# Row length of five zero fills on the software DMA queue: fills 25, 26, 27, 29 and 30 written in 56 KB rows

## The chip, the cores and the metric

One core of one Trainium2 chip. The metric is the device time of one execution in microseconds (us), less is better. Six runs of the kernel before lie between 766.58 and 799.4 us, with a median of 774.3 us.

## What is computed

The program is the forward and backward pass of one decode step: a layer norm, an attention block A over a sliding window of a key/value cache, a gate from a small dense block B with a squared ReLU, and `x + s * g`; the outputs are the result and the gradients of all inputs.

```python
W = min(4096, max(256, Sk // 4))           # Sk = 32768, so W = 4096
k = jnp.repeat(k_cache[:, :, Sk - W:, :], rep, axis=1)
v = jnp.repeat(v_cache[:, :, Sk - W:, :], rep, axis=1)
p = _softmax(scores, axis=-1)
...
s = _A_ref(xn, A_k_cache, A_v_cache, A_wq, A_wo)
g = _silu(_B_ref(xn, B_w1, B_b1, B_w2, B_b2))
return x + s * g
```

Only the last 4,096 of 32,768 cache rows are used. The gradients of both caches (`out_2`, `out_3`; 2 batches x 8 heads x 32,768 rows x 128 bf16 each) are therefore zero in the first 28,672 rows of each head. These zeros are 32 pieces of 7.34 MB, 234.9 MB in all, out of 280.50 MB that the program writes.

## The kernel before

**Zero fills.** `zt` (line 80) is a tile of 128 x 14,336 bytes of zeros. The helper `zf` (line 90) writes one piece, or a part of it, from that tile by a DMA on POOL's software queue (line 101), and lets the DMA convert the bytes on the way: the destination is read as bf16, so that one tile row becomes 28,672 bytes of output, or, where a row would be longer than the tile's, as fp32, so that one tile row becomes 57,344 bytes. The loop at line 115 issues pieces ("fills") 0 to 30 in order of number. A fill whose number is in `zlong` (line 107) is written in 128 rows of 57,344 bytes ("long"); one that is not is written in 256 rows of 28,672 bytes ("short"); fills 2, 4, 6, 8 and 10 are cut into parts of several sizes by `zshort` (line 108). In the order of the queue, the last ones are: 16 to 19 long, 20 and 21 short, 22 to 24 long, 25 to 27 short, 28 long, 29 and 30 short. They make 47 DMAs. The queue has eight semaphores, so POOL issues a DMA when the one eight places before it has landed; the last one is issued at 553.65 us of the profile, and the queue is never empty before that. Fill 31 is written at the very end, by SP (line 623): it is issued after SP's last other store and waits for the landing of fill 29 (line 624).

**Attention.** After the weights, four rounds (the loop over `rounds`, two groups of four heads x two batches) each hold a V tile and a K tile of 4 MB, in one buffer each. A round computes scores with V and K (`scores`, lines 377 and 383), the softmax, the contractions (`contract`, line 399), then the gradients tile by tile *into the same buffer* (`outer_store`, line 410), and stores that buffer on ACT's queue (line 414): first V's, then K's. SP loads the next round's V (line 213) once V's store has landed, and K likewise. K and V rows go in 32,768-byte pieces, 128 of them to a tile. In the second and fourth rounds the gradient of `wq` is also formed, in place (line 495).

**Epilogue.** Line 498 gives the K/V buffers back, and the tiles of the epilogue (`epi`, line 499) are placed there: so `o_rows`, the first of them, is written only after the last K store has landed. The epilogue is one chain of small steps: `o_rows` (line 506), the output projection (line 515), the gate, the gradients of B (lines 555 to 590), then `dw2` (line 608) and its store on SP (610), `dw1` (616) and its store (618), fill 31 (623), and the gradient of `wo` (628) and its store on ACT's queue (630). The gradient of `wq` is stored by ACT at line 500.

Of the kernel before, what the change touches and what calls it, by code (L numbers as in the profile page):

```python
# [16 lines left out]
def kernel(  # L17
# [86 lines left out]
    ZQ = 2 * B * HKV  # L104
    zparts = [(out_2, q) for q in range(B * HKV)] + [(out_3, q) for q in range(B * HKV)]

    zlong = (3, 5, 7, 11, 12, 16, 17, 18, 19, 22, 23, 24, 28)
    zshort = {
        2: ((5, 8, 2), (120, 68, 3), (128, 32, 1), (16, 1, 1)),
        4: ((3, 1, 2), (2, 99, 6), (128, 112, 1), (128, 102, 1), (86, 1, 1)),  # L110
# [547 lines left out]
```

## Time and profile before

| what | value |
|---|---|
| six runs: times | 766.58, 766.74, 766.74, 781.86, 784.45, 799.4 us |
| six runs: median | 774.3 us |
| the profiled execution: its own time | 800.91 us |
| the profiled execution: span, first to last instruction | 799.1 us |
| PE, DVE, ACT, POOL busy | 415.2 (52%), 277.2 (35%), 214.9 (27%), 30.2 us (4%) |
| bytes moved by DMA | 326.73 MB, mean 409 GB/s |
| of these by the software queue | 227.55 MB in 8000 packets |
| last V store: issued, landed | 648.61, 684.57 us |
| last K store: issued, landed | 677.56, 702.66 us |
| store of `dw2` issued | 758.53 us |
| fill 31 issued, landed | 765.90, 796.94 us |

The profile is one execution, the longest of those listed. Times in it are counted from its first instruction. A "packet" is one piece that a DMA engine moves in one go; in this trace a packet of the fills is one row (28,672 or 57,344 bytes), and one of the K and V transfers is 32,768 bytes. Sixteen DMA engines serve all queues: q0 is POOL's software queue, q1 is SP's, q10 is ACT's. The page cuts the span in 40 slices of 20 us; the digits are tenths of busy time, and the row GB/s is what the DMA engines moved in each slice.

### The profile page before, as it was taken

The page shows a single profiled execution, that of the slowest core. Times are in us where ns is not written, and L with a number is a line of the kernel's source. Part 1 is how long each engine was busy: PE and PEld are TensorE (multiplying, and loading weights), DVE is VectorE, ACT ScalarE, POOL GpSimd, SP SyncE. Part 2 cuts the span into 40 slices and gives each one's busy share as a digit, 9 for nine tenths or more (in the row PEclk, how much of TensorE's full clock was granted, in tenths as well). Part 3 has the DMA queues.
Part 4 walks back from the last instruction along what each step waited for, and adds up shares of the span by engine and source line. Part 5 has one row for each costly group of instructions (what it writes and reads, how often), then busy time and mean ns, then how long its engine had stood idle before and what let it go on. Part 6 is the DMA issues. An engine that isn't in the chain of part 4 may idle for free.

```text
span 799.1 us, 9402 instructions
## 1 busy us (share of the span) xinstructions
PE 415.2 (52%) x4118; PEld 269.3 (34%) x4118; DVE 277.2 (35%) x484; ACT 214.9 (27%) x313; POOL 30.2 (4%) x56
## 2 busy tenths in 40 slices
PE   0275873747503757750583578102517587275690
PEld 0253462634102645420362443002516443134230
DVE  3034241355401437440141375201204554113770
ACT  0024431145500235450120256100102465120260
POOL 3000000010000100000000000000000000000000
PEclk9997897868755996675576968655959587556555
DMA  9999999999999999999999999999999999993089
GB/s 358 433 432 418 444 422 434 423 450 412 429 431 435 428 437 424 427 433 434 436 435 437 428 419 433 432 438 429 442 418 431 429 443 420 434 432 150 1 367 394
DMA packets 12473, 326.73 MB, mean 409 GB/s; under 512 B 2276, under 2 KB 2284, under 8 KB 2294
## 3 DMA queue, kind: packets, MB, share of 16 engines
q0 software_dynamic: 8000, 227.55, 67.3%
q1 hardware_dynamic: 2696, 56.63, 19.9%
q10 hardware_dynamic: 1736, 41.95, 12.4%
q8 instruction: 32, 0.52, 0.2%
q14 instruction: 9, 0.07, 0.0%
HBM read 45.62 MB, written 280.50 MB: 408 GB/s over the span
## 4 chain that ended last, share of the span: by engine, by line
DMA 37%; PE 32%; DVE 13%; ACT 7%; issue 4%; another core or an unknown queue 3%; ACTq 0%; DVEq 0%; SPq 0%
DMA out_dram<-nat 14%; DMA nat<-in_A_k_cache_dram 10%; DMA nat<-in_A_v_cache_dram 9%; PE ov L410 6%; PE s_ps L383 4%; PE tp L377 4%; DMA b_bf<-in_B_b_dram 4%; DVE tT L156 3%; PE dp_ps L383 2%; ACT p_bf L444 2%; DVE nat L156 2%; PE wps L628 2%; DVE ds_bf L457 2%; ACT tT L154 2%
## 5 line engine op out<-in xcount | busy, mean ns | idle before, releaser
L377 PE MATMUL tp<-pperm,nat 128*128 128x128 bf16 x1024 | 85.0, 234 | 175.7 <-DMA nat<-in_A_v_cache_dram 122.5
L156 DVE COPY tT<-tp 128x1024 bf16<-128x1024 bf16 x96 | 64.1, 689 | 242.1 <-PE tp L377 241.5
L377 PEld LDWEIGHTS <-nat 128*128 128x128 bf16 x1024 | 74.1, 106 | 182.2 <-DMA nat<-in_A_v_cache_dram 124.2
L154 ACT COPY tT<-tp 128x1024 bf16<-128x1024 bf16 x32 | 32.4, 1012 | 305.7 <-PE tp L377 305.7
L154 ACT CAST nat<-ov 128x512 bf16<-128x512 f32 x160 | 87.9, 589 | 60.9 <-PE ov L410 59.6
L156 DVE CAST nat<-ov 128x512 bf16<-128x512 f32 x96 | 65.4, 690 | 57.7 <-PE ov L410 56.9
L410 PE MATMUL ov<-bd,ds_bf 128*128 128x512 bf16 x128 | 52.2, 486 | 5.8 <-DVE nat L156 3.9
L410 PE MATMUL ov<-bd,p_bf 128*128 128x512 bf16 x128 | 47.4, 438 | 4.7 <-DVE nat L156 1.8
L383 PE MATMUL dp_ps<-tT,zdo 128*128 128x256 bf16 x256 | 42.2, 298 | 14.5 <-DVE tT L156 8.6
L101 POOL DMA_DIRECT2D out_dram<-zt x47 | 28.6, 613 | 524.1 <-DMA out_dram<-zt 520.8
L383 PE MATMUL s_ps<-tT,zq 128*128 128x256 bf16 x256 | 39.4, 280 | 13.9 <-DVE tT L156 9.2
L383 PEld LDWEIGHTS <-zdo 128*128 128x128 bf16 x256 | 25.8, 105 | 23.4 <-issue 19.8
L399 PE MATMUL ps<-t,nat 128*128 128x16 bf16 x1024 | 28.5, 173 | 9.4 <-DVE bd L367 7.8
L399 PEld LDWEIGHTS <-nat 128*128 128x128 bf16 x1024 | 28.4, 101 | 12.7 <-issue 7.6
L383 PEld LDWEIGHTS <-zq 128*128 128x128 bf16 x256 | 24.7, 100 | 20.9 <-issue 18.2
L495 PE MATMUL wps<-dq_rows,xn_bf 2*128 2x512 bf16 x32 | 14.9, 536 | 23.2 <-ACT wq L154 18.0
L391 PE MATMUL tp<-ident_bf,p_bf 128*128 128x128 bf16 x64 | 7.6, 313 | 34.9 <-ACT p_bf L444 34.9
L444 ACT ACTIVATE p_bf<-e_sb,rl 32x512 bf16<-32x512 f32 x16 | 22.8, 1423 | 3.4 <-DVE rl L441 3.3
L156 DVE CAST wq<-wps 128x512 bf16<-128x512 f32 x16 | 11.0, 690 | 31.6 <-PE wps L495 31.2
L457 DVE SCALAR_TENSOR_TENSOR ds_bf<-dp_ps,delta,p_bf 32x512 bf16<-32x512 f32 x16 | 21.7, 1358 | 0.2
L410 PEld LDWEIGHTS <-ds_bf 128*128 128x128 bf16 x128 | 13.6, 113 | 23.0 <-issue 20.7
L154 ACT CAST dw_st<-wps 128x512 bf16<-128x512 f32 x15 | 8.8, 585 | 46.4 <-PE wps L608 43.7
(197 smaller groups left out, 454.7 us busy)
## 6 DMA issues: line engine op xcount, KB each, us to landing
out_dram<-zt POOLq DMA_DIRECT2D x26, 7168.0 KB, 162.4
out_dram<-nat ACTq DMA_DIRECT2D x8, 4096.0 KB, 32.9
nat<-in_A_v_cache_dram SPq DMA_DIRECT2D x4, 4096.0 KB, 34.1
nat<-in_A_k_cache_dram SPq DMA_DIRECT2D x4, 4096.0 KB, 38.2
out_dram<-zt POOLq DMA_DIRECT2D x4, 3584.0 KB, 56.6
out_dram<-zt SPq DMA_DIRECT2D x1, 7168.0 KB, 31.0
out_dram<-zt POOLq DMA_DIRECT2D x1, 6120.0 KB, 85.9
wo<-in_A_wo_dram SPq DMA_DIRECT2D x1, 4096.0 KB, 38.3
```

The lines of the kernel that those rows point to most:

```text
L101: sw_fill.append(nc.gpsimd.dma_start(out=v, in_=zs))
L154: nc.scalar.copy(out=out_ap, in_=in_ap)
L156: nc.vector.tensor_copy(out=out_ap, in_=in_ap)
L377: nc.tensor.transpose(tp[:, j, :], nat[:, g * CC + half * CH + j, :], pperm[:].rearrange("p b k -> p (b k)"))
L383: nc.tensor.matmul(out_ps[:, half * CH * PB:(half + 1) * CH * PB], lhsT=zbuf[:, pr, o:o + R], rhs=tT[:, :, pr, :], start=(g == 0 and pr == ...
L391: nc.tensor.transpose(tp[:, cc, :], src[:, half * CH + cc].rearrange("r k b -> r (k b)"), ident_bf[:, :])
L399: nc.tensor.matmul(ps[:], lhsT=nat[:, g * CC + half * CH + cc, :], rhs=cols[half][:, cc, :, g, :], start=(half == 0 and g == 0 and cc == 0 ...
L410: nc.tensor.matmul(ov[:], lhsT=src[:, cc].rearrange("r k b -> r (k b)"), rhs=bd[:, gh * 4:(gh + 1) * 4, :], start=True, stop=True)
L444: nc.scalar.activation(out=p_bf[rb, :, :, pr], in_=e_sb[rb], func=ACT.Copy, scale=rl[rb, 0:1])
L457: nc.vector.scalar_tensor_tensor(out=ds_bf[rb, :, :, pr], in0=dp_c[rb], scalar=delta[rb, 0:1], in1=p_bf[rb, :, :, pr], op0=ALU.subtract, o ...
L495: nc.tensor.matmul(wps[:], lhsT=xn_bf[:, k:D:DK], rhs=dq_rows[:, :], start=True, stop=True)
L628: nc.tensor.matmul(wps[:], lhsT=o_rows[:, j:N:NJ], rhs=ds_rows[:, :], start=True, stop=True)
```

## The change

Five numbers are added to the tuple of long fills; nothing else is touched.

```diff
-    zlong = (3, 5, 7, 11, 12, 16, 17, 18, 19, 22, 23, 24, 28)
+    zlong = (3, 5, 7, 11, 12, 16, 17, 18, 19, 22, 23, 24, 25, 26, 27, 28, 29, 30)
```

For these five, `whole` at line 117 is `(128, 224, 1)` in place of `(128, 112, 2)`: one DMA each as before, of 128 rows of 57,344 bytes in place of 256 rows of 28,672. All fills from 22 to 30 are then long. The number of DMAs, their order, their semaphores, and the instructions of all other engines stay as they are; fill 31 still waits for fill 29.

## The prediction

> **What bounds the kernel now.** I read the page's 40 slices first, then busy times by stage, the DMA queues in short windows, the chain of work that ended last, and the waits. The slices:
>
> ```profile
> DMA  9999999999999999999999999999999999993089
> GB/s 358 433 432 418 444 422 434 423 450 412 429 431 435 428 437 424 427 433 434 436 435 437 428 419 433 432 438 429 442 418 431 429 443 420 434 432 150 1 367 394
> ```
>
> The DMA engines are full from 20 us to about 727 us at some 430 GB/s; then comes one hole, which the stages show (columns: busy us and count for PE, PEld, DVE, ACT, POOL, then PE clock, DMA share, GB/s):
>
> ```profile
> 597.00:648.00 51.00, 36.84 (x417) 26.83 (x416) 27.00 (x44) 22.20 (x31) 0.00 (x0) 0.80 1.03 435
> ...
> 728.00:758.00 30.00, 18.94 (x178) 11.32 (x176) 17.77 (x27) 4.10 (x7) 0.52 (x1) 0.50 0.01 2
> 758.00:800.00 42.00, 20.94 (x48) 6.55 (x47) 15.78 (x25) 14.04 (x24) 0.00 (x0) 0.50 0.85 362
> ```
>
> The hole is 30 us with 2 GB/s: the fills are used up, and the epilogue has not yet made what is left to store. The execution took 800.9 us; without the hole it would be about 771. That lies near the lowest three of the six runs (766.6 to 766.7, within 0.2 us of each other), so I read those as runs without a hole: DMA engines full to the end, and nothing to gain but bytes. The other three (781.9, 784.5, 799.4) have holes of 15 to 33 us. The time is the later of two ends: that of the bytes, 766.7, and that of the chain.
>
> Where the chain comes from, before the hole:
>
> ```profile
> 677.56 25.10 DMA out_dram<-nat
> 702.76 1.00 ACT o_rows L154
> ```
>
> ```profile
> ACT o_rows L154 <- DMA out_dram<-nat: 19.4, 1, 19.4
> ```
>
> The first epilogue step stands 19.4 us, until the last K store (issued 677.56) has landed at 702.66. From there, small steps follow without another DMA wait to the `dw2` store at 758.53 (55.9 us) and on to the end. So each us that this store lands later makes the hole, where there is one, a us longer.
>
> [...] Beside short fills, the last V store, and the last K store:
>
> ```profile
> q10 hardware_dynamic: 111, 3.54, 55.9%
> q0 software_dynamic: 109, 2.84, 44.4%
> ```
>
> ```profile
> q10 hardware_dynamic: 112, 3.67, 57.4%
> q0 software_dynamic: 112, 2.87, 44.8%
> ```
>
> (windows 664 to 679 and 685 to 700 us; packets, MB, share). 111 packets against 109, 112 against 112: one for one. Beside long fills, the last K load, 556 to 576 us:
>
> ```profile
> q0 software_dynamic: 96, 5.33, 62.1%
> q1 hardware_dynamic: 98, 3.21, 38.4%
> ```
>
> Again one for one, but now the fill takes 62% of the bytes. [...] the one issued at 544.09 landed at 596.77, 52.7 us later. [...]
>
> **The change, part by part.**
>
> *Fewer rows (removed).* 5 x 128 = 640 packets fewer. Fills that run alone show what a row length is worth: POOL's issues at 422.93, 439.68, 456.56, 473.48 and 490.42 mark the landings of fills 16 to 20. The long ones 17, 18, 19 took 16.75, 16.88 and 16.92 us, the short fill 20 took 16.94. At best 5 x 0.19 = 1 us, at worst nothing; I take 0. POOL's issue is 0.54 us for a long fill against about 0.71 for a short one, 0.9 us less over five, hidden: POOL stands 520.8 us waiting for landings.
>
> *Fills 25, 26, 27.* In this execution they run from 597 to 648 us, where the window shows 435 GB/s and the queue listing q0 alone. No other transfer competes: cost 0. Their cover is that the last round's loads have landed (596.77). If the chain runs some 25 us earlier, as it must where there is no hole, the last V store would start beside fill 26 or 27 instead of 28, and meet long rows there; the next two steps then apply a little earlier, at the same price.
>
> *Fill 29, beside the last V store.* The store moved nothing from 649 to 660 us, behind rows of fill 28, which is long already. From 664 it had 3.54 MB left, taking 15 us at 0.236 MB/us. Beside long rows the measured pace is 3.21/20 = 0.160 MB/us: 22.1 us, so 7 us later; last bytes at about 687 in place of 679.7.
>
> *Fills 29 and 30, beside the last K store.* It sits behind the V store on ACT's queue. Before, its first packet moved at 683.4; now it waits until 687: 3.7 us later. Its 4.19 MB took 4.19/0.245 = 17.1 us at 3.67/15; at 0.160 they take 26.2: 9.1 more. Fills 29 and 30 together, 14.7 MB at 5.33/20 = 0.267 MB/us from 664, last until 719, so they accompany the store to its end. Sum: 3.7 + 9.1 = 12.8 us. The late semaphore, which stores have shown as up to 4.9 us after the last packet, may add 0 to 5; a queue delay that is lighter than the pace of a load suggests may take off 4. I take 12, with bounds 8 and 18; a gain is excluded here, since no packet of a store moves sooner when those between are longer.
>
> *After that.* The landing goes to about 715, and all of the epilogue moves with it: `dw2` at 770, the end at 813 for the execution profiled. The `wq` store (issued 711.13) moves too, but finds no fill beside it, so it ends before `dw2`; 0. Fill 31 waits for fill 29, which lands earlier than before; SP reaches it only after the `dw1` store, so this frees nothing. No wait or instruction is added on PE, DVE, ACT or SP.
>
> **From the profiled execution to the median.** Runs with a hole pay all 12 us: 781.9 becomes 793.9, 784.5 becomes 796.5, 799.4 becomes 811.4. Runs at the floor pay what exceeds their slack, the time by which their chain ends early. No profile of such a run is here; slack is between 0 and, from the spread of the six, some 25 us. If it is 8 us, they go to 770.7. The median of six is then the middle of 770.7 and 793.9: 782 us.
>
> **Rivals.**
>
> *A, slack covers it (not slower).* In runs at the floor the chain may end over 12 us early; then the stores give up bytes to the fills and get them back at the end, the total being fixed, and the time stays 766.7. It decides from a slack of 12 us. For it: three runs within 0.2 us, which a chain close to the floor would have scattered. Against it: the other three are 15 to 33 us above, so the chain's own scatter is wider than the slack can be sure of. Time where most runs are at the floor: 767.
>
> *B, longer rows move more bytes (faster).* The 1 us above, or a hole that the fills' earlier end makes no longer. Faster by over 0.2% needs 1.5 us, more than the five fills can give by the rows measured. Only a floor that sinks, or a sample with fewer holes, would show it: 765.5.
>
> *C, late landing decides (much slower).* The load that landed 52.7 us after its issue was beside long rows. If the last stores, or in a late run the last K load beside fill 25, land some 10 us later yet, the median is 782 + 10 = 792, and single runs pass 815.
>
> That the change does nothing is no rival: the 13 long fills are in the trace with 57,344-byte packets by the same code.
>
> **Chances.** 0.2% (1.5 us) is about what a measurement can tell here. My forecast (some us up to 12) 0.52; C 0.12; A 0.28; B 0.08. So slower 0.64, same 0.28, faster 0.08. The range goes from A's floor, 766, to 798, which takes in most of C; about 1 in 10 is left out above and 1 in 10 below. The slower cases alone would give 770 to 798.
>
> **What would show it.** Right: beside fills 29 and 30 the q0 share near 62% and q10 at 0.16 MB/us; last K store 33 to 38 us from issue to landing in place of 25.10; ACT's wait at `o_rows` longer by that; a longer DMA hole, or a new one. Wrong: `o_rows` not waiting for the store, or a full DMA row up to the last slice with the stores late (A).

## The result and the profile after

The changed kernel takes 816.67 us in the median of 10 runs (799.12 to 818.3); the kernel before takes 774.34 us in the median of 20 (766.58 to 801.34). Over the runs of each kernel that lie within 1.5% of its fastest, the ratio is 1.0433, 95% interval [1.0418, 1.0448]: 33 us slower. The runs of both kernels fall in groups some 17 us apart (766.7, 783 and 800 before; 799 to 801 and 814 to 818 after). The execution profiled after belongs to the lower group (798.84 us, span 797.1), and the fourth round's K load lands at 562.8 us in it. So its fair partner is not the profile of 800.91 us that the prediction read, where that load lands at 596.77, but one of the kernel before at 766.96 us (`b_look1`), where it lands at 563.2.

The slices of the changed kernel's page:

```profile
DMA  9999999999999999999999999999999999994089
GB/s 357 434 429 425 434 434 433 420 443 417 436 430 429 437 437 415 438 426 429 436 439 435 430 423 426 430 435 436 440 432 433 423 434 421 446 424 189 1 368 395
```

and those of the kernel before in the run of 766.96 us:

```profile
DMA  9999999999999999999999999999999999999998
GB/s 356 429 429 427 443 416 429 444 424 425 427 435 430 430 445 435 418 425 432 432 433 441 427 430 428 430 432 433 437 435 431 419 432 432 435 428 425 427 429 367
```

The prediction read the lowest runs as runs without a hole, and so it is. The change puts a hole of some 30 us in. Two stretches of the changed kernel, the second being the hole (columns as before):

```profile
649.00:701.00 52.00, 5.69 (x39) 2.54 (x39) 4.70 (x9) 2.98 (x5) 0.00 (x0) 0.53 1.29 431
728.00:755.00 27.00, 17.56 (x164) 10.64 (x161) 15.95 (x25) 3.51 (x6) 0.00 (x0) 0.50 0.01 1
```

In the first of these 52 us every compute engine is nearly idle while the DMA engines are full: the epilogue waits for the last K store. The waits of the changed kernel, and of the kernel before at 766.96 us:

```profile
ACT o_rows L154 <- DMA out_dram<-nat: 47.2, 1, 47.2
```

```profile
ACT o_rows L154 <- DMA out_dram<-nat: 20.4, 1, 20.4
```

The chain that ended last, of the changed kernel from 590 us on:

```profile
600.92 6.00 issue
...
633.63 5.33 issue
...
654.11 47.08 another core or an unknown queue
701.29 1.00 ACT o_rows L154
```

and of the kernel before at 766.96 us:

```profile
638.62 25.47 DMA out_dram<-nat
664.19 1.00 ACT o_rows L154
```

Two things are new: two stretches in which PE waits for nothing that the profile shows ("issue", 11.3 us; the kernel before at 766.96 us has none of over 2.0 us), and the 47.08 us before `o_rows`, for which the chain names no cause. The last K store was issued at 648.94 and landed at 701.19. Its packets say where the time went. The table gives, from the trace's records, the time from issue to first packet, from there to the last packet (of the 128 of 32,768 bytes), and from that to landing, with the V store ahead of it on the same queue:

| store | issued | to first packet | packets move | last packet to landing | in all |
|---|---|---|---|---|---|
| last V, before, 800.91 us | 648.6 | 12.1 | 19.0 | 4.9 | 36.0 |
| last V, before, 766.96 us | 617.2 | 6.5 | 18.4 | 2.7 | 27.7 |
| last V, changed, 798.84 us | 621.0 | 12.0 | 25.0 | 4.8 | 41.8 |
| last K, before, 800.91 us | 677.6 | 5.9 | 18.1 | 1.2 | 25.1 |
| last K, before, 766.96 us | 638.6 | 5.6 | 18.5 | 1.4 | 25.5 |
| last K, changed, 798.84 us | 648.9 | 11.0 | 24.7 | 16.5 | 52.2 |

The V store is the clean measure of the start: nothing stands ahead of it on ACT's queue. When the K store was issued, the V store still moved, for another 2.1, 3.5 and 9.1 us in the three executions.

So the account of the lower groups, both counted from the landing of the fourth round's K load (563.2 and 562.8 us): V store issued 54.0 and 58.2 us later (+4.2), K store 21.5 and 28.0 after that (+6.5), landed 25.5 and 52.2 after that (+26.7), `dw2` 56.7 and 55.3 after that (-1.4). Sum +36.0; the times differ by 31.9, so some 4 us were slack. The +26.7 are 5.4 of start, 6.2 of moving packets and 15.1 of wait after the last packet.

The shares beside long rows, in windows 636 to 656 and 664 to 684 us of the changed kernel (V store, K store):

```profile
q0 software_dynamic: 98, 4.87, 56.7%
q10 hardware_dynamic: 108, 3.54, 42.5%
```

```profile
q0 software_dynamic: 109, 5.45, 63.2%
q10 hardware_dynamic: 107, 3.51, 41.8%
```

Still about one packet each (98 against 108, 109 against 107), and 3.51/20 = 0.176 MB/us for the store, near the 0.160 of the forecast.

### The profile page after: what moved, and what is told of

Same layout as the page of the kernel before. It is cut to its first block, busy times and chain, and to the rows that moved or that the text cites. A ratio compares the mean times of both kernels' runs of the same rounds, so it can differ in the third digit from the quotient of the medians.

```text
span 797.1 us, 9402 instructions
## 1 busy us (share of the span) xinstructions
PE 413.9 (52%) x4118; PEld 269.2 (34%) x4118; DVE 277.1 (35%) x484; ACT 214.7 (27%) x313; POOL 29.3 (4%) x56
## 4 chain that ended last, share of the span: by engine, by line
PE 32%; DMA 32%; DVE 15%; ACT 8%; another core or an unknown queue 6%; issue 5%; ACTq 0%; DVEq 0%; SPq 0%
DMA out_dram<-nat 11%; DMA nat<-in_A_k_cache_dram 9%; DMA nat<-in_A_v_cache_dram 8%; PE ov L410 5%; PE s_ps L383 4%; PE tp L377 4%; DMA b_bf<-in_B_b_dram 4%; DVE tT L156 3%; PE dp_ps L383 3%; DVE ds_bf L457 2%; ACT p_bf L444 2%; DVE nat L156 2%; PE wps L628 2%; PE dops L308 2%
## 5 line engine op out<-in xcount | busy, mean ns | idle before, releaser
L410 PE MATMUL ov<-bd,ds_bf 128*128 128x512 bf16 x128 | 49.8, 468 | 5.7 <-DVE nat L156 4.1
L410 PE MATMUL ov<-bd,p_bf 128*128 128x512 bf16 x128 | 49.7, 457 | 4.1 <-DVE nat L156 1.8
L383 PE MATMUL dp_ps<-tT,zdo 128*128 128x256 bf16 x256 | 41.3, 294 | 15.2 <-DVE tT L156 8.4
L101 POOL DMA_DIRECT2D out_dram<-zt x47 | 27.7, 594 | 534.4 <-DMA out_dram<-zt 531.2
L383 PEld LDWEIGHTS <-zdo 128*128 128x128 bf16 x256 | 25.5, 104 | 23.9 <-issue 20.6
L156 DVE CAST wq<-wps 128x512 bf16<-128x512 f32 x16 | 11.0, 690 | 58.6 <-PE wps L495 58.2
L483 PEld LDWEIGHTS <-wqT 128*128 128x128 bf16 x128 | 4.4, 101 | 52.1 <-issue 50.7
```

What stands on the lines that cost most here:

```text
L101: sw_fill.append(nc.gpsimd.dma_start(out=v, in_=zs))
L156: nc.vector.tensor_copy(out=out_ap, in_=in_ap)
L383: nc.tensor.matmul(out_ps[:, half * CH * PB:(half + 1) * CH * PB], lhsT=zbuf[:, pr, o:o + R], rhs=tT[:, :, pr, :], start=(g == 0 and pr == ...
L410: nc.tensor.matmul(ov[:], lhsT=src[:, cc].rearrange("r k b -> r (k b)"), rhs=bd[:, gh * 4:(gh + 1) * 4, :], start=True, stop=True)
```

## Experiments

In the traces of both kernels the records of a K or V store end with 16 packets of 4 bytes, called its completion writes here; the last K store of the changed kernel has 14 that took 12.7 to 14.8 us, the last of them ended at 700.85 us, the store landed at 701.19, and fill 29, in flight beside it, at 701.90. "Held" is said below of a completion write that lasts so long. Three theories, for the runs to test: **S** (the forecast's): only the shares of bytes count. **H1**: a completion write beside a long fill is held until that fill's DMA has ended. **H2**: it is held only as long as nothing else follows on its own queue. What the long fills have that the others lack is also split: the length of the row, or the conversion of the zeros to fp32 (each byte of the tile becomes four of output, called widening by 4; by 2 in a short row).

**e0_before_again**: the kernel before, no edit.

> The kernel before, unchanged, to see a run at the floor (766.7 us). Theory H (a load's or store's completion write is held until the long fill in flight has ended, up to 7 packets of 2.11 us): in such a run the last round runs some 25 us earlier than in the profile of before, the last K store starts near 645 to 650 us beside fill 27 or 28, and its landing comes at 670 to 680; the dw2 store is issued within some 5 us of the end of the fills and of the wq store (about 728), so there is little slack. Theory S (only the shares of bytes count, and the slack is used up by more than the forecast 12 us): the chain in a run at the floor ends close to the floor, slack 0, and the last K store takes 25 to 30 us.

Measured: 766.69 to 801.29 us in five runs; the profile is of the run of 801.29 and shows what the first profile showed, so it leaves the slack open. It shows where the group at 800 comes from, though: the fourth round's K load has its last packet at 581.6 us and lands at 596.8, with fill 24 (597.0).

**e1_long_25_27 and e2_long_29_30**: one part of the change each.

```diff
-    zlong = (3, 5, 7, 11, 12, 16, 17, 18, 19, 22, 23, 24, 28)
+    zlong = (3, 5, 7, 11, 12, 16, 17, 18, 19, 22, 23, 24, 25, 26, 27, 28)
```
```diff
+    zlong = (3, 5, 7, 11, 12, 16, 17, 18, 19, 22, 23, 24, 28, 29, 30)
```

> Fills 25, 26 and 27 long, 29 and 30 short. Theory H: the last K store lands while a short fill runs, or at the end of fill 28, so the wait after its last packet falls from 16.5 us to under 2 where fill 29 runs then; runs at about 780 to 788 us, 12 to 19 less than the changed kernel's lower runs (799). Theory S: the last V and K stores move beside fills 25 to 28 for most of their bytes, so most of the loss stays: 790 to 799 us.

> Fills 29 and 30 long, 25 to 27 short. Theory H: if the last K store's last packet moves during fill 28 or 29, its completion is held until that fill ends: landing near 700 us and runs near 795 to 800 us, though most of its bytes moved beside fills of before. Theory S: the V store is as quick as before, the K store only little slower: 770 to 778 us.

Measured: e1 784.57, 792.62, 801.39, 801.6 us; e2 782.86, 799.24, 816.14, 816.93. Against the lowest run of before, both parts cost about 17 us in theirs, and the whole about 32; but four runs can miss a group. In e1's profile (801.6) the last K store moves beside the short fill 29 and lands 23.9 us after its issue, as quickly as before, and PE stands 5.64 us in "issue" beside fill 27: the V store, issued 51.8 us after the K load's landing in the profile of before, is issued after 57.9. In e2's (816.14) that store takes 42.3: 12.3 to the first packet, 27.9 moving, 2.0 to land, at the very end of the fills (718.2, fill 30 at 718.4). S has e2 at 770 to 778 and fails for every run; H1's 795 to 800 holds for one of four. The parts do not act on the same thing: with 25 to 27 long, PE stops and the V store is issued later (57.9 us against 51.8), with 29 and 30 long the K store takes longer (42.3 us against 25.1).

In both profiles the fourth round's K load lands at 596.8 us, as in the profile of 800.91 us, so that is their partner. Beside it e1 costs 0.7 us: its V store starts sooner after its issue (10.1 us in place of 12.1), and the K store is issued 2.0 us later only. e2 costs 15.2, and nearly all of that is what the forecast counted: the V store moves 8.9 us longer, the K store starts 6.5 and moves 9.9 longer. In e2's profile the loss lies in when the packets start and how long they move, not in the 2.0 us after them.

**e3_f32_short**: the five fills in rows of 28,672 bytes, as before the change, but converted to fp32.

```diff
-    def zf(o, q, r0, nent, rows, rep=1):
+    def zf(o, q, r0, nent, rows, rep=1, as_f32=False):
...
-        if w > ZG * DH:
+        if as_f32 or w > ZG * DH:
...
-            r = zf(*zparts[qi], r, n, rows, rep)
+            r = zf(*zparts[qi], r, n, rows, rep, as_f32=qi in (25, 26, 27, 29, 30))
```

> The five fills in rows of 28,672 bytes as before, but converted to fp32 as the long ones are (7,168 bytes of the tile a row). If row length decides (H and S as stated): as the kernel before, 766.7 us in its lower runs. If the conversion to fp32 is what holds completions: the last K store lands up to 7 packets of 1.06 us late, so 774 to 780 us, with completion writes of several us in the trace.

Measured: 799.09, 799.14, 801.32, 818.33 us: the changed kernel's times, with the rows of the kernel before, and far from both expectations. So most of the loss comes with the conversion, not with the length. The equal times are in part chance: in e3's profile the K load lands at 574.5 us, 11.7 later than in the changed kernel's, and both K stores land with the end of fill 29, at 701.8 and 701.2. The V store beside these rows starts 11.9 us after its issue (12.0 in the changed kernel, 6.5 in the kernel before at 766.96 us), a time in which each engine moved some 11 packets of the fill instead of 5 or 6 (estimates: 167 packets on 16 engines in the 11 us from 632 in e3, 2.16 us for a long packet in the changed kernel, 1.08 for a short one); the K store's completion comes 13.3 us after its last packet (1.4 in the kernel before at 766.96 us); PE stands 5.34 and 4.04 us in "issue". Only the share is another matter; windows 672 to 687 us of e3, K store beside fp32 rows of 28,672 bytes:

```profile
q10 hardware_dynamic: 100, 3.28, 52.0%
q0 software_dynamic: 104, 3.01, 46.9%
```

3.28/15 = 0.219 MB/us, with about one packet each: the store's share goes with the row's length, as the forecast had it (52.0% here, 55.9 and 57.4% beside rows of this length in the kernel before, 41.8% beside 57,344 bytes in the changed kernel); the waits at both ends go with the conversion (11.9 and 13.3 us).

**e4_push and e4_look**: the changed kernel, with a small load right behind the last K store on ACT's queue.

```diff
+    push = const.tile([P, FK], BF16, name="push")
...
+        if r == NR - 1:
+            with tc.issue_after(st.ins):
+                dma_store.dma_start(out=push[:], in_=B_b1.rearrange("(p j) -> p j", j=FK))
```

> The changed kernel, with one small load (128 pieces of 28 bytes of B_b1, into a tile that nothing reads) issued on ACT's queue right after the last K store. Theory H2 (a completion write beside fp32 fills is held while nothing else follows on its queue, and passes after one or two fill packets if something does, as the last V store's did with the K store behind it): the K store's wait after its last packet falls from 16.5 us to 3 to 6, so 784 to 789 us in the lower runs (799 for the changed kernel). Theory H1 (it is held until the fp32 fill in flight has ended, whatever follows): no change, 799 and 817 us.

> The changed kernel with the small load behind the last K store, one look. Theory H2 (traffic behind a completion lets it pass): in a run at 789 to 792 us the wait after the last K store's last packet is under 7 us, where the changed kernel has 16.5. Theory H1 alone: a run at 799 us with 13 to 17 us of wait.

Measured: e4_push 789.51, 791.88, 817.23, 817.28 us; its profile (817.23) tells nothing of the hold, since there the K store lands at the end of all fills (719.1). e4_look's profile is of a run of 785.75 us: the wait after the last packet is 3.3 us where the changed kernel has 16.5, with fill 29 in flight until 702.3 and the landing at 688.3. So here, with something behind it on its queue, the store landed 14.0 us ahead of the fill. The last V store shows the same without any edit: in the changed kernel, with the K store's packets starting behind it, 14 of its 16 completion writes took 2.16 us, as long as one long packet (2.16); 14 of the 16 of the K store, with nothing behind it, took 12.7 to 14.8, as long as six or seven.

H2 as worded is wrong at two points, though. To stand in the queue was not enough in b_look2: the fourth round's K load was issued behind the V load at 542.7 us, its first packet moved at 551.0, and the V load's completion writes took up to 12.7 us and ended between 549.1 and 553.1, with fill 22. And the other transfer was not on the same queue in another case: in six profiles the third round's K store ended beside a long fill with nothing behind it, while a load moved on SP's queue (at 540.3 us in the profile of 800.91 us), and its completion writes took 0.01 us.

The profile of 817.23 us tells something else: its K load lands at 596.8 us, as in the profile of 800.91. So with the fills long a run of the group at 800 comes out at 817, 16 us later and not 33.

**e5_two_halves**: the changed kernel, each of the five fills as two DMAs of 64 long rows.

```diff
+        if qi in (25, 26, 27, 29, 30):
+            whole = (P // 2, ZR // P, 1)
...
-    tc.add_manual_dep(fin.ins, sw_fill[-2].ins.name,
+    tc.add_manual_dep(fin.ins, sw_fill[-3].ins.name,
```

Fill 31 waits for the second half of fill 29.

> The changed kernel, with each of the five fills as two DMAs of 64 long fp32 rows, so that a DMA has 4 packets on an engine instead of 8. Theory H1 (held until the end of the fill DMA in flight): at most 3 to 4 packets of 2.11 us are held, 6 to 8 us instead of 14.8, so about 791 us in the lower runs. [...]

Measured: 789.66, 799.7, 800.14, 817.59 us. In the profile (789.66) the K store's last packet ends at 684.6 and the store lands at 692.1, with the first half of fill 29 (692.8): 7.5 us instead of 16.5, and the completion writes took at most 6.4 us, three packets (14.8 in the changed kernel). This is H1's number, with 4 packets a DMA and engine in place of 8.

**e6_short_from_20**: all fills from 20 on short.

```diff
+    zlong = (3, 5, 7, 11, 12, 16, 17, 18, 19)
```

> All fills from 20 on in short bf16 rows, 22, 23, 24 and 28 too. If the fp32 fills 22 to 24 hold the fourth round's K load until a fill's end, and so set by how much each run exceeds 766.7 us, then all runs are at 766.7 us, and the trace shows how early the chain ends: the fourth round's K load lands by 560 us, the last K store at 655 to 665, dw2 at 715 or before. If the scatter of the runs comes from elsewhere, runs near 783 and 800 us remain.

Measured: 12 runs at 766.72 to 770.34 us, median 766.93; ratio to the kernel before 1.0008 [0.9997, 1.0018]. The fourth round's K load lands 1.1 us after its last packet, at 562.5; last K store landed 658.9; `dw2` issued at 715.7. Its slices show no hole:

```profile
GB/s 359 428 423 434 435 424 430 440 426 426 432 431 427 434 438 435 416 428 436 430 430 447 432 430 421 429 432 433 432 427 430 430 432 429 432 432 429 427 427 370
```

So with the fills from 22 on short the groups at 783 and 800 us of the kernel before did not show in 12 runs. In the two groups that have profiles the K load's completion came with the end of fill 22 (766.96 us) and of fill 24 (800.91 and 801.29); the middle group has none. This version is no quicker than the kernel before at its best (766.72 against 766.58 us).

**e8_plain**: the five fills without conversion, bf16 zeros to bf16, in rows of 14,336 bytes.

```diff
+        zs = (zt[:].bitcast(BF16) if plain else zt)[0:nent * st:st, 0:w].unsqueeze(1).to_broadcast([nent, rep, w])
...
+        if plain:
+            whole = (P, ZG // 2, 2 * ZR // (P * ZG))
```

> The five fills without any conversion: bf16 zeros from a bf16 source, 128 x 4 rows of 14,336 bytes. Theory R ([...] 5.5 us from issue to first packet with widening by 2, 11 to 12 with widening by 4, whatever the row): the last V or K store beside fills 25 to 30 starts 3 to 4 us after its issue, and takes 70% of the bytes by packet (32,768 to 14,336). Times as the kernel before or a little better where a fill of 22 to 24 does not decide: 766.7 in the lower runs. Theory P (the delay is some 5 packets): 3.5 us too, but then e3's 28,672-byte rows should have given 5.5, and gave 11.9.

Measured: 766.74 to 793.06 us, median 767.04 of 14, ratio 1.0 [0.9989, 1.0011]. The last V and K stores start 3.7 and 3.9 us after issue; here the V store had ended when the K store was issued. With widening by 1, 2 and 4 the start of a store that has none ahead of it took 3.7 to 3.9 us (e8), 6.5 (the kernel before at 766.96 us) and about 12 (changed kernel and e3), the last with both row lengths. A store that met idle DMA engines started after 0.83 us (`dw2` in the profiles of 800.91 and 798.84 us). Why the start grows with the widening is not shown. The share moves with the row again (V store, window 631 to 645 us):

```profile
q10 hardware_dynamic: 131, 3.96, 66.2%
q0 software_dynamic: 136, 1.92, 32.1%
```

The K store's completion, though, fell beside fill 28, which is long here too, and came 14.1 us after its last packet.

**c1_base and c2_long25**: the change alone, on a base that has fills 22 to 24 short, so that the fourth round's K load is not held by them.

```diff
+    zlong = (3, 5, 7, 11, 12, 16, 17, 18, 19, 28)
```
```diff
+    zlong = (3, 5, 7, 11, 12, 16, 17, 18, 19, 25, 26, 27, 28, 29, 30)
```

> A base without the scatter: the kernel before with fills 22, 23 and 24 in short bf16 rows, so that the fourth round's K load is not held; 25 to 27, 29 and 30 short, 28 long, as before. Theory H1 (a completion is held until the fp32 fill DMA in flight has ended): all runs at 766.7 to 770 us; the last K store is issued near 634 to 640 us and lands at 660 to 680, beside fill 28 or before it.

> The same base with the change made on it: 25 to 30 long. Theory H1: the last K store's packets end before 685 us and its completion is held to the end of fill 28 or 29 (685 or 702), the later of them if the packets end after 685; PE stands 5 to 6 us more for instructions; runs at 783 or at 799 us, all in one or two groups 17 us apart, no others. Theory S (shares alone, 12 us): 766.7 to 772 us, since the base has some 12 us of slack.

Measured: c1 eleven runs at 766.66 to 767.05 us and one at 783.59 (the profiled one); c2 782.43, 783.58, 800.08, 800.73; ratio of c2 to the kernel before 1.0213 [1.0183, 1.0243]. S has c2 at 766.7 to 772 and fails again. Neither profile is of a run at the floor, but they pair well, with the K load landed at 574.5 and 574.1 us: V store issued after 52.6 and 58.0 us, K store after another 21.2 and 26.4, landed after 36.7 and 43.2. c2's chain from 600 us on:

```profile
611.59 6.97 issue
...
644.22 4.25 issue
```

c1's has no such entry of over 0.76 us. These 11 us account for the later issue of both stores (5.4 and 5.2 us). The groups at 783 and 800 are those that H1 names. This pair does not show the hold, though: the last packet to landing is 7.2 us in c1, beside the long fill 28, and 3.1 in c2, where the packets end just ahead of fill 29's end. The 6.5 us more to landing are +7.0 of start, +3.7 of moving packets and -4.1 of hold.

That K load landed 11.9 and 11.8 us after its last packet, beside short fills, which H1 does not foresee: one of its 16 completion writes took 12.85 us, in both. It ended at 574.05 and 573.67 us, at the same moment as one completion write of a fill. c3 and c4 below show it too, with 5.4 and 7.5 us. So beside short fills one of the 16 was late in these four profiles; why not the others is open.

**c3_push**: c2_long25 with the small load behind the K store, as in e4.

> c2_long25 with the small load right behind the last K store on ACT's queue. Theory H2 (traffic behind it on the queue lets the completion pass): the wait after the last packet falls from up to 15 us to under 5, and the runs fall to 770 to 785 us. Theory H1 alone: as c2_long25.

Measured: 20 runs from 767.08 to 801.32 us, median 777.88 (c2: 791.83), seven of them at 767.1 to 767.6. In the profile (779.75) the completion comes 6.7 us after the last packet, before fill 28's end (680.8 against 685.1), not under the 5 expected. The fills are those of c2, whose lowest of four runs is 782.43. So in the seven at the floor the slack covers all that the long fills add besides the hold: the later start, the pace and the stops of PE. Four runs at about 800 are left, which no profile here shows.

**c4_eighths**: c2_long25 with each fill from 25 on as eight DMAs of 16 long rows.

```diff
+        if qi >= 25:
+            whole = (P // 8, ZR // P, 1)
...
-    tc.add_manual_dep(fin.ins, sw_fill[-2].ins.name,
+    tc.add_manual_dep(fin.ins, sw_fill[-9].ins.name,
```

Fill 31 waits for the last part of fill 29.

> c2_long25 with each fill from 25 on as eight DMAs of 16 long fp32 rows: the same packets of 57,344 bytes and the same widening, but one packet per engine in a DMA. Theory H1: the hold is at most one or two packets (2 to 4 us), the delay before the first packet stays at 11 to 12 us [...]; runs at 770 to 780 us. [...]

Measured: 774.91, 775.17, 776.34, 777.94 us. The K store's completion comes 2.5 us after its last packet and no completion write beside these fills takes over 1 us: the hold is gone, with rows and conversion in place, and with 10.8 us to the V store's first packet. This is H1's number again. The runs are still 8 us above 766.9. The chain is later than in b_look1: fill 31 is issued at 739.89 us against 728.17, 11.7 later, of which some 4 were slack, so the chain gives the 8. The row GB/s shows where the engines have less to do at the end:

```profile
GB/s 358 431 433 420 449 421 423 433 436 422 429 431 435 429 447 425 420 431 433 433 439 424 443 428 419 432 431 430 432 430 445 423 425 430 429 412 434 301 363 395
```

Beside the many small DMAs they also moved a little less, 404 GB/s from 680 to 700 us and 410 and 416 in the two windows of 10 us after, where the row of b_look1 has 425 to 429.

**b_look1 and b_look2**: the kernel before, no edit.

> The kernel before, one look, to catch a run at 766.7 us. If the forecast was right on slack (8 us): dw2 issued some 8 us before the end of the fills and of the wq store. If the chain ends close to the floor: dw2 issued within 4 us of it (about 724 to 729 us). In both, the last K store takes 24 to 30 us from issue to landing.

> A second look at the kernel before, with the same expectations as the first.

Measured: 766.96 and 799.47 us. The first is the partner used above. SP's queue in it:

```profile
720.80 0.33 SPq L610 DMA_DIRECT2D out_dram<-dw_st  x1
727.79 0.33 SPq L618 DMA_DIRECT2D out_dram<-dw_st  x1
728.17 0.43 SPq L623 DMA_DIRECT2D out_dram<-zt  x1
```

Fill 30 lands at 729.9, so `dw2` is issued 9 us ahead of the end of the fills, and fill 31 less than 2. The forecast's slack of 8 us for `dw2` was about right; what counts to the end is nearer 4, as the account above has it.

## Why the prediction was wrong, step by step

The sign and the place were right: the last K store lands later, `o_rows` waits for it, and the delay comes out as a hole. The size was right only for the group of the profile that was read. A run at 800.91 us was to end at 813; those with the same landing of the K load end at 816.14 (e2, fills 29 and 30 alone) and 817.23 (e4_push, all five and the small load), and there the store lands 2.0 and 0.5 us after its last packet. The lower runs were to pay the same 12 us or, at the floor, less, and end at 770.7. In the pair at 766.96 and 798.84 us the chain is 36 us later instead: 10.7 before the K store's issue, 5.4 of start, 6.2 of moving packets, 15.1 of wait after the last packet, 1.4 less after that. The range ended at 798.

*"The late semaphore, which stores have shown as up to 4.9 us after the last packet, may add 0 to 5."* This is the step that failed, in the runs of the lower group. It was 16.5 us, 15.1 more than in the kernel before at 766.96 us. The loads had shown the size (the K load of 52.7 us, of which 15.5 passed after its last packet), and rival C took it up, with some 10 us and a chance of 0.12. But the sum took a store for another kind of thing than a load. What told them apart in the profile of before was not their direction: of the eight K and V stores, seven ended beside short fills, and the eighth, at 540.3 us, while a load moved on SP's queue. The 16.5 us of the changed kernel became 7.5 with fewer packets in a DMA (e5) and 3.3 with something behind the store on its queue (e4_look); on the base with fills 22 to 24 short it was 2.5 with fewer packets (c4) and 6.7 with something behind (c3), where c2 itself has 3.1, its packets ending just ahead of fill 29's end. Why a completion write is held stays open. The length and the widening of the rows alone do not set it: c4 has the rows of the changed kernel in both.

*"Fills 25, 26, 27."* The second term put at nothing: *"No other transfer competes: cost 0."* The V and K stores were issued 10.7 us later. No K or V transfer runs beside these fills in the profile read, but q0 was not alone in its listing of 597 to 648 us:

```profile
q0 software_dynamic: 799, 22.13, 102.6%
q8 instruction: 3, 0.05, 0.4%
```

Queue q8, "instruction" on the page, moved pieces of 16,384 bytes, and in the traces of both kernels, c2, e1 and e3 one such piece moves inside each stop of PE named here (at 604.48 and 636.45 us in the changed kernel). PE stood 6.00 and 5.33 us in the changed kernel, and 6.97 and 4.25 in c2 against none in c1. e3 has such stops with short rows (5.34 and 4.04 us). These pieces were not varied, so that PE waited for them is the author's guess and not shown. Such a stop stood in the chain of the profile read, beside the long fill 28, with a piece of q8 moving at 664.0 us:

```profile
662.07 4.41 issue
```

The longer start of the V store is the third such term: 12.0 us in place of 6.5. In the profile read it was 12.1 already, since that V store met the long fill 28, so the sum for a run where it meets fill 26 or 27 left it out.

*The pace beside long rows* held: 7 us and 9.1 us were forecast for the V and K stores' packets; they took 6.6 and 6.2 more (8.9 and 9.9 in e2). *"3.7 us later"* at the K store's start was near (5.4), with the cause it named: its first packet came 1.9 us after the V store's last, and 2.1 in the kernel before at 766.96 us.

*Slack* of 8 us was close (4 to 9). *That runs with a hole pay the same* did not hold: the lowest group pays 32 us, the group at 800 some 16. Runs at 814 to 818 after can come from the groups at 783 and at 800 before; which, the changed kernel's one profile doesn't show. *Rival A* fell with the size. *Rival B* fell: no run of the changed kernel is faster than any of the lowest group before. *Rival C* had the cause and was too small: a median of 792, where 816.67 was measured. *Fewer rows: 0* stands: from 600 to 616 us, with no K or V transfer, short fills moved 427 GB/s (b_look1) and long ones 428 (changed kernel).

The deeper mistake: the change was read as one of row length, because that is what the code says. The long rows differ in two ways, and the one that the text of the change does not name, the conversion to fp32, costs most: e3, without longer rows, has no run below 799.

## What to carry to other kernels

The long fills here cost the stores beside them more than bytes: 12.0 us to the V store's first packet in place of 6.5, and 16.5 us from the K store's last packet to its landing in place of 1.4. So time from issue to landing should be split in three (start, packets, completion) before a cost is put on it. Where a transfer's landing opens the next step, try fills that widen less beside it (e8: a median of 767.04 us), or DMAs of fewer packets (c4: 2.5 us from last packet to landing), or another transfer behind it on its queue (e4_look: 3.3 us). And read a second execution of another group before a delay found in one is carried to all. A change that alters two properties at once is to be costed for each of them, the stops of other engines included (11.3 us of PE here).

## What the runs showed of the hardware that was not expected

- From issue to first packet, a K or V store with none ahead of it on its queue took 3.7 and 3.9 us beside fills without conversion (e8), 6.5 beside fills that widen by 2 (b_look1, e6, c1) and 11.8 to 12.3 beside fills that widen by 4 in most profiles, with rows of 28,672 (e3, 11.9) and 57,344 bytes (changed kernel, 12.0) alike. c4 (eight DMAs a fill) gave 10.8, e1 10.1.
- A store's completion write of 4 bytes took up to 14.8 us, as long as seven fill packets of 2.11 us, and the store landed at 701.19 us, with the fill beside it (701.90; changed kernel). It took at most 6.4 us with four packets a DMA and engine (e5), under 1 us with one (c4). It took at most 2.2 to 4.3 us where other packets followed on the same queue (changed kernel's V store, e4_look, c3), and 0.01 us where a load moved on another queue (third round's K store, six profiles). Why is open. It was not tried whether the same happens with bf16 rows of 57,344 bytes.
- In equal times a store and a fill moved nearly the same number of packets at each row length here: 131 against 136 at 14,336 bytes (e8), 100 against 104 at 28,672 (e3), 107 against 109 at 57,344 (changed kernel).
